# Dealing two rows of a weight matrix instead of one to the first few DMA engines, in a decode kernel on one core

## The chip, the core and the metric

The kernel runs on one core of one Trainium2 chip. The metric is the device time of one execution in microseconds (us), the median of several runs. Details below come from one execution that the hardware profiler recorded; its time axis starts with the first instruction of the program ("the span's start").

A core has five instruction streams: TensorE (PE in the profile, with its weight loads as PEld), VectorE (DVE), ScalarE (ACT), GpSimd (POOL) and SyncE (SP). DMA transfers are issued from SP and ACT here and are carried by the core's sixteen DMA engines, each of which works through its own share of every transfer.

## The reference: what is computed

A decode step for a batch of 8 tokens of width 512. An attention branch over a window of 2048 cached keys and values (8 key/value heads of 128, 32 query heads), and a gated unit whose result, once more through a gate, multiplies it:

```python
xn = layernorm(x)
s  = attention(xn @ wq, k_cache[:, :, -2048:], v_cache[:, :, -2048:]) @ wo
h  = sigmoid(xn @ w_gate) * (xn @ w_up)       # 8 x 1792
g  = silu(h @ w_down)                         # w_down: 1792 x 512
out = x + s * g
```

All inputs are bf16. The two caches' windows are 64 MB together, the weights about 13.5 MB; every byte is read once.

## The kernel before, in words

**One stream of loads.** Nearly all loads go through SP's queue `q0`, in an order that is written out by hand: the lists `todo` and `room` (lines 104 to 132) hold the tiles that are wanted and the buffers that are left, and `pump` issues a load as soon as its pool has room. The order is: x, `w_gate` (half of it on ACT's queue), `w_up`, `w_down` as tile `wd_sb`, `wq` in two tiles, the rest of `w_down` as `wd_part`, then 16 tiles of keys and 16 of values of 2 MB each (`k_sb`, `v_sb`), and last `wo` in five pieces of 12, 8, 6, 4 and 2 rows per partition (line 205). Each full load spreads its 128 partitions over the sixteen DMA engines, eight partitions to an engine. Keys and `wq`, `wo` share a pool of five buffers, values and the gated unit's weights one of four.

**The last weights of the gated unit.** `w_down` has 1792 rows of 512 bf16, 1 KB each. Seen as (p r) with 14 rows to a partition, rows 1 to 13 of every partition are loaded as one tile of 13 KB per partition (`want_rows("wd_sb", ..., FT, SD, FT)`, line 194, SD = 1). Row 0 of every partition, 128 rows in all, is loaded on its own by `want_part` (lines 179 to 192) into `wd_part`, a tile of 64 partitions x 3 rows in the values' pool. GpSimd first zeroes the tile (L183); then three transfers (L187) fill it, described by `PARTS` (lines 175 and 176): two with 60 rows whose source has 5 as its outermost size, and one with 8 rows and 4 outermost. The three are called "the dealt rows" below.

**The gated unit in order of work.** `hidden` (line 291) makes gate and up projections on PE; h_sb (L312) and its 32x32 transposed hT_sb (L320) follow on DVE. As the dealt rows lie on other partitions than the rest, h has to be put on those partitions too: three matmuls with 0/1 matrices `sel_part` (L327; made on DVE at L277 and L280) give hP_ps, and L335 copies it to hP_sb. Then 16 matmuls (L348) add up h @ w_down into w_ps, 13 on `wd_sb` and three on `wd_part`, in four row groups of PE by turns. The tail of that branch is L358 to L375. PE then makes q (L385, L404) and starts on the keys.

**Attention.** For each of 16 key tiles PE transposes 64 blocks (L481), DVE copies them out of PSUM (L486), PE makes the scores (L500); softmax, the turning of the probabilities (L571) and the products with the values (L597) are woven in by the table `tasks` (line 658). The output projection comes last: 20 rows of `wo` through part_ps (L719), then into fin_ps (L733); DVE multiplies and adds (L748, L750), SP stores the result (L751).

Of the kernel before, what the change touches and what calls it, by code (L numbers as in the profile page):

```python
# [10 lines left out]
def kernel(  # L11
# [13 lines left out]
    nc = tc.nc  # L25
    P = 128
    B, _, D = A_x.shape
    _, Hkv, Sk, Dh = A_k_cache.shape
# [20 lines left out]
    bf16 = mybir.dt.bfloat16  # L49
    f32 = mybir.dt.float32  # L50
# [8 lines left out]
    vpool = ctx.enter_context(tc.tile_pool(name="vpool", bufs=4))  # L59
    ktpool = ctx.enter_context(tc.tile_pool(name="ktpool", bufs=3))  # L60
    ppool = ctx.enter_context(tc.tile_pool(name="ppool", bufs=2))
    consts = ctx.enter_context(tc.tile_pool(name="consts", bufs=1))
    work = ctx.enter_context(tc.tile_pool(name="work", bufs=1))
    small = ctx.enter_context(tc.tile_pool(name="small", bufs=2))
    ps_t = ctx.enter_context(
        tc.tile_pool(name="ps_t", bufs=4, space=bass.MemoryType.PSUM)
    )
# [6 lines left out]
    ps_m = ctx.enter_context(  # L74
        tc.tile_pool(name="ps_m", bufs=1, space=bass.MemoryType.PSUM)
    )
    ctx.enter_context(tc.manual_schedule())


# [27 lines left out]
    def later(tag, f):  # L107
        todo.append((tag, f))
# [11 lines left out]
    def want_rows(name, w, tag, per, r0, r1):  # L120
        def f():
            t = load_rows(w, tag, per, r0, r1, name)
            for r in range(r0, r1):
                weights[(name, r)] = t[:, r - r0, :]

        later(tag, f)
# [13 lines left out]
    Z = 32  # L140
# [26 lines left out]

    A = 5  # L170
    SD = 1
    SX = 3
    HP = P // 2
    NA = 4 * A
    PARTS = ((0, NA, 0, SX, 0, A), (Z, NA, 0, SX, SX * NA, A))
    PARTS += ((Z + NA, P - 2 * SX * NA, 0, 1, 2 * SX * NA, 4),)
    d_room = []

    def want_part(w, per):
        def f():  # L180
            d = vpool.tile([HP, SX, SD, w.shape[1]], bf16, name="wd_part", tag="v")
            d_room.append(d)
            nc.gpsimd.memset(d[:], 0.0)  # L183
            for p0, n, x0, x1, s0, a in PARTS:
                m = n * (x1 - x0)
                src = w.rearrange("(y r) n -> y (r n)", r=per)[s0 : s0 + m]
                q0.dma_start(  # L187
                    out=d[p0 : p0 + n, x0:x1].rearrange("p x r n -> p (x r n)"),
                    in_=src.rearrange("(y a) n -> a y n", a=a)[:, :, : SD * w.shape[1]],
                )  # L190

        later("v", f)

    want_rows("wd_sb", B_w_down, "v", FT, SD, FT)
    for i in range(2):
        want_rows("wq_sb", A_wq, "k", KT, 2 * i, 2 * i + 2)
    want_part(B_w_down, FT)
    order = [(b, i) for b in range(B) for i in range(NQ)]
    AHEAD = 3
# [5 lines left out]
    for t0, t1 in ((0, 12), (12, KS), (KS, 26), (26, 30), (30, RT)):  # L205
# [4 lines left out]
    ident = consts.tile([P, P], bf16, name="ident")  # L210
# [6 lines left out]
        out=perm[:].rearrange("k (l p) -> k l p", l=G),  # L217
        in_=ident[:].rearrange("k (p l) -> k l p", l=G),
# [13 lines left out]
        out=rstd[:], in_=mv[:, 1:2], func=AF.Sqrt, bias=eps_t[:], scale=1.0  # L232
# [4 lines left out]
        out=xn_bf[:],  # L237
# [8 lines left out]
    for kt in range(KT):  # L246
        nc.tensor.transpose(  # L247
            out=xnT_ps[:, kt, :],
            in_=xn_bf[:].rearrange("b (p kt) -> b kt p", kt=KT)[:, kt, :],
# [11 lines left out]
    for t in p_buf:  # L261
        nc.vector.memzero(t[:])
    oP_sb = work.tile([P, RT, Z], bf16, name="oP_sb")
    nc.vector.memzero(oP_sb[:])

    NDQ = Dh // RT
    own_q = consts.tile([P, NDQ], f32, name="own_q")
    nc.vector.reduce_sum(
        out=own_q[:], in_=ident_f[:].rearrange("k (h q) -> k q h", q=NDQ), axis=AX.X
    )  # L270
    sel_z = consts.tile([P, Z], f32, name="sel_z")
    nc.vector.reduce_sum(
        out=sel_z[:], in_=ident_f[:].rearrange("k (j z) -> k z j", z=Z), axis=AX.X
    )

    sel_part = consts.tile([P, SX, HP], bf16, name="sel_part")
    nc.vector.memzero(sel_part[:])  # L277
    for p0, n, x0, x1, s0, a in PARTS:
        for x in range(x0, x1):
            nc.vector.tensor_copy(  # L280
                out=sel_part[:, x, p0 : p0 + n].rearrange("k (a e) -> k a e", a=a),
                in_=ident[:, s0 : s0 + n * (x1 - x0)].rearrange(
                    "k (e x a) -> k x a e", x=x1 - x0, a=a
                )[:, x - x0],
            )

    FC = F // NB

    def hidden(name):
# [21 lines left out]
        out=h_sb[:].rearrange("k t p -> k p t"),  # L313
# [5 lines left out]
    hT_sb = work.tile([P, FT, Z], bf16, name="hT_sb")  # L319
    nc.vector.transpose(  # L320
        out=hT_sb[:].rearrange("k t z -> k (t z)"),
        in_=h_sb[:].rearrange("k t p -> k (t p)"),
    )

    hP_ps = ps_t.tile([HP, SX, SD * Z], f32, name="hP_ps", tag="t")
    for x in range(SX):
        nc.tensor.matmul(  # L327
            hP_ps[:, x, :],
            lhsT=sel_part[:, x, :],
            rhs=hT_sb[:, :SD, :].rearrange("p t z -> p (t z)"),  # L330
            start=True,
            stop=True,
        )
    hP_sb = work.tile([HP, SX, SD * Z], bf16, name="hP_sb")
    nc.vector.tensor_copy(out=hP_sb[:], in_=hP_ps[:])  # L335
    down = [(hT_sb[:, t, :], weights[("wd_sb", t)]) for t in range(SD, FT)]
    for x in range(SX):
        top = max(p0 + n for p0, n, x0, x1, _, _ in PARTS if x0 <= x < x1)
        down += [
            (hP_sb[:top, x, Z * r : Z * (r + 1)], d_room[0][:top, x, r, :])  # L340
            for r in range(SD)
        ]

# [2 lines left out]
    for t, (h, w) in enumerate(down):  # L346
# [3 lines left out]
            lhsT=h,  # L350
            rhs=w,
            start=(t < NB),
            stop=(t >= len(down) - NB),
            tile_position=(0, Z * j),
            skip_group_check=True,
# [4 lines left out]
    for j in range(NB):  # L360
        nc.tensor.matmul(
            b_ps[Z * j : Z * (j + 1), :],
            lhsT=sel_z[:],
            rhs=w_sb[:, 0, j * P : (j + 1) * P],
            start=True,
            stop=True,
            tile_position=(0, Z * j),
            skip_group_check=True,
# [12 lines left out]
    for kt in range(KT):  # L381
        for x in range(Hkv // JQ):
            for j in range(JQ):
# [3 lines left out]
                    lhsT=xnT_sb[:, kt, :],  # L387
                    rhs=weights[("wq_sb", kt)][:, g * rep * Dh : (g + 1) * rep * Dh],
                    start=(kt == 0),
                    stop=(kt == KT - 1),  # L390
                    tile_position=(0, Z * j),
                    skip_group_check=True,
# [3 lines left out]
    for x in range(Hkv // JQ):  # L396
        src = q_ps[x][:].rearrange("k (r d) -> k r d", r=rep)
# [4 lines left out]
    for x in range(Hkv // JQ):  # L402
        for r in range(rep):
            nc.tensor.transpose(  # L404
                out=qT_ps[:, x, r, :], in_=q_bf[:, x, r, :], identity=ident[:]
            )
        nc.vector.tensor_copy(
            out=qm_sb[:, :, x * JQ : (x + 1) * JQ, M0 : M0 + rep],
            in_=qT_ps[:, x].rearrange("d r (j z) -> d z j r", z=Z)[:, ::S],
# [11 lines left out]
    for i in range(NQ):  # L421
        nc.vector.tensor_copy(
            out=turn_rows[:].rearrange("k (i j l r) -> k i j l r", i=NQ, j=NJ, l=G)[
                :, i
            ],
            in_=ident[:].rearrange("k (l j i r) -> k i j l r", i=NQ, j=NJ, l=G)[:, i],
        )
        nc.vector.reduce_sum(
            out=sel_den[:, i * Hh : (i + 1) * Hh].rearrange("k (l r) -> k l r", l=G),
            in_=ident_f[:].rearrange("k (l j i r) -> k i l r j", l=G, j=NJ, i=NQ)[:, i],  # L430
            axis=AX.X,
        )
    for e in range(2):
        nc.vector.reduce_sum(
            out=sel_out[:, e, :].rearrange("k (i h) -> k i h", i=NQ),
            in_=ident_f[:].rearrange(
                "k (i m e h) -> k e i h m", i=NQ, m=NJ // 2, e=2
            )[:, e],
# [6 lines left out]

    sel_res = consts.tile([P, Hq, NDQ], f32, name="sel_res")
    nc.vector.tensor_tensor(
        out=sel_res[:],
        in0=sel_out[:, 0, :].unsqueeze(2).to_broadcast([P, Hq, NDQ]),
        in1=sel_out[:, 1, :].unsqueeze(2).to_broadcast([P, Hq, NDQ]),  # L450
        op=ALU.add,
    )
    sel_sum = consts.tile([P, Hq, NDQ], f32, name="sel_sum")
    nc.vector.tensor_copy(
        out=sel_sum[:], in_=sel_den[:].unsqueeze(2).to_broadcast([P, Hq, NDQ])
# [261 lines left out]
    for t in range(KS):  # L717
# [3 lines left out]
            lhsT=oP_sb[:, t, :],  # L721
            rhs=weights[("wo_sb", t)],
            start=(t < NB),
            stop=(t >= KS - NB),
            tile_position=(0, Z * j),
            skip_group_check=True,
# [16 lines left out]
    for t in range(KS, RT):  # L743
# [8 lines left out]
        out=out.flatten_outer_dims().rearrange("b (j c) -> j b c", c=P),  # L752
        in_=y_bf[::S, :],
# [31 lines left out]
```

## Time and profile before

| what | value |
|---|---|
| median of 3 runs | 199.87 us (199.56 to 200.12) |
| the profiled execution, its own time | 199.72 us |
| its span, first to last instruction | 198.0 us |
| outside the span | 1.7 us |
| TensorE clock granted, mean | 0.972 of full speed |
| PE busy | 152.7 us, 77% of the span, 2133 matmuls |
| DVE busy | 122.2 us, 62% |
| ACT busy | 37.6 us, 19% |
| POOL busy | 3.0 us, 1% |
| bytes moved by DMA | 81.32 MB, a mean of 411 GB/s |

The page's chain of work that ended last gives DMA 57% of the span and PE 34%. The busy share of PE is a mean over stages: for the first 34 us it waits mostly for weights.

Besides instructions, the trace keeps each DMA packet (start, duration, bytes, queue) and each update of a semaphore. A packet here is one contiguous run of bytes of a transfer on one DMA engine. A transfer tells that it has landed by one update of its semaphore from each DMA engine that carried a part of it, after that engine's last packet; the instruction that needs the data waits for all of them. The packets' records don't name the engine, but on one engine each begins 3 to 4 ns before the one ahead of it ends, so that sixteen strands can be followed through the whole run. Times of packets and of landings differ by a constant: a landing is seen about 0.3 us after the packet.

### The profile page before, as it was taken

What the parts mean: (1) busy time and instruction counts of PE and PEld (TensorE: products, weight loads), DVE (VectorE), ACT (ScalarE), POOL (GpSimd) and SP (SyncE); (2) the same over time, 40 slices, a digit from 0 to 9 for tenths busy, and PEclk for the clock granted to TensorE, in tenths of its full rate; (3) what the DMA queues carried; (4) which work ended last, traced back from release to release, by engine and by line L of the source; (5) the groups of instructions that cost most, each with busy time, mean ns of one, the idle gap of its engine ahead of it and who ended that gap; (6) DMA issues with size and microseconds to landing.
All of it is one profiled execution on the core that took longest, in us unless ns stands there. A gap on an engine that the chain in (4) does not pass through costs nothing.

```text
span 198.0 us, 4772 instructions
## 1 busy us (share of the span) xinstructions
PE 152.7 (77%) x2133; PEld 103.3 (52%) x2133; DVE 122.2 (62%) x234; ACT 37.6 (19%) x91; POOL 3.0 (1%) x11
## 2 busy tenths in 40 slices
PE   0434038799979999989798969996989797898552
PEld 0111014677666677656565646674657565566421
DVE  3764002999978679758675937687858674852301
ACT  3200011000720610240024000600140033082010
POOL 5000000000000000000000000000000000000000
PEclk9999999999999999999999969999999999999975
DMA  6999999999999999999999999999999999999980
GB/s 207 433 438 428 428 443 427 434 424 422 430 427 434 427 434 427 427 430 427 427 427 435 427 430 430 422 434 424 430 427 434 427 434 430 427 424 422 421 341 10
DMA packets 6441, 81.32 MB, mean 411 GB/s; under 512 B 782, under 2 KB 918, under 8 KB 1558
## 3 DMA queue, kind: packets, MB, share of 16 engines
q1 hardware_dynamic: 6242, 80.10, 95.0%
q10 hardware_dynamic: 180, 0.93, 1.4%
q8 instruction: 16, 0.26, 0.5%
q14 instruction: 3, 0.02, 0.0%
HBM read 81.02 MB, written 0.01 MB: 409 GB/s over the span
## 4 chain that ended last, share of the span: by engine, by line
DMA 57%; PE 34%; ACT 3%; DVE 3%; SPq 1%; issue 1%
DMA k_sb<-in_A_k_cache_dram 33%; PE kT_ps L481 17%; DMA wo_sb<-in_A_wo_dram 11%; DMA wd_part<-in_B_w_down_dram 10%; PE o_ps L597 6%; PE s_ps L500 5%; DMA wg_sb<-in_B_w_gate_dram 3%; ACT p_buf L548 2%; PE pT_ps L571 2%; PE q_ps L385 1%; DVE kT_sb L486 1%; SPq L99 1%; ACT L548 1%; PE fin_ps L733 1%; PE qT_ps L404 0%
## 5 line engine op out<-in xcount | busy, mean ns | idle before, releaser
L486 DVE COPY kT_sb<-kT_ps 128x1024 bf16<-128x1024 bf16 x128 | 85.1, 686 | 30.8 <-PE kT_ps L481 30.1
L481 PE MATMUL kT_ps<-perm,k_sb 128*128 128x128 bf16 x1024 | 75.8, 221 | 10.1 <-DMA k_sb<-in_A_k_cache_dram 10.1
L481 PEld LDWEIGHTS <-k_sb 128*128 128x128 bf16 x1024 | 59.1, 99 | 29.8 <-issue 16.2
L597 PE MATMUL o_ps<-v_sb,pT_sb 128*32 128x256 bf16 x512 | 39.7, 276 | 1.6 <-DVE o_sb L618 0.9
L500 PE MATMUL s_ps<-kT_sb,qm_sb 128*32 128x512 bf16 x256 | 25.8, 393 | 1.9 <-DVE kT_sb L486 1.9
L597 PEld LDWEIGHTS <-pT_sb 128*32 128x32 bf16 x512 | 21.9, 96 | 10.2 <-issue 3.5
L548 ACT ACTIVATE p_buf<-s_ps,nb 32x512 bf16<-32x512 f32 x32 | 21.7, 678 | 0.5
L541 ACT COPY nb<-m_ps 128x1 f32<-128x1 f32 x8 | 1.3, 159 | 87.0 <-PE m_ps L535 87.0
L571 PE MATMUL pT_ps<-turn_rows,p_buf 128*128 128x128 bf16 x128 | 10.9, 230 | 1.5 <-ACT p_buf L548 1.5
L564 DVE COPY pT_sb<-pT_ps 128x1024 bf16<-128x1024 bf16 x14 | 9.6, 687 | 3.9 <-PE pT_ps L571 3.9
L500 PEld LDWEIGHTS <-qm_sb 128*32 128x32 bf16 x256 | 6.7, 93 | 8.8 <-issue 2.4
L571 PEld LDWEIGHTS <-p_buf 128*128 128x128 bf16 x128 | 9.3, 150 | 3.4 <-ACT p_buf L548 2.1
L613 ACT ACTIVATE o_odd<-o_ps,own_col 128x128 f32<-128x128 f32 x8 | 2.9, 368 | 28.5 <-PE o_ps L597 28.4
L375 DVE TENSOR_TENSOR gg_sb<-sigb,b_ps 128x128 f32<-128x128 f32 x1 | 0.3, 289 | 12.0 <-ACT sigb L371 12.0
L348 PE MATMUL w_ps<-wd_part,hP_sb 52*32 52x512 bf16 (+1 forms) x3 | 0.6, 597 | 8.1 <-DMA wd_part<-in_B_w_down_dram 8.1
L548 ACT ACTIVATION_READ_ACCUMULATOR p_buf<-s_ps,nb 32x1 f32 x32 | 5.9, 184 | 0.0
L515 DVE TENSOR_REDUCE st<-s_ps 128x1 f32<-128x512 f32 x8 | 5.5, 681 | 0.5 <-PE s_ps L500 0.5
L618 DVE SCALAR_TENSOR_TENSOR o_sb<-o_ps,own_col,o_odd 128x128 f32<-128x128 f32 x8 | 2.7, 339 | 3.5 <-ACT o_odd L613 3.5
L348 PEld LDWEIGHTS <-hP_sb 52*32 52x32 bf16 (+1 forms) x3 | 0.1, 97 | 9.0 <-issue 9.0
L640 DVE SCALAR_TENSOR_TENSOR own<-m_ps,inv,own_q 128x128 f32<-128x128 f32 x8 | 2.8, 346 | 3.1 <-PE m_ps L631 3.1
L247 PE MATMUL xnT_ps<-ident,xn_bf 8*128 8x8 bf16 x4 | 0.3, 174 | 5.4 <-DVE xn_bf L236 5.4
L295 PEld LDWEIGHTS <-xnT_sb 128*32 128x32 bf16 x32 | 1.1, 119 | 6.3 <-issue 5.8
(80 smaller groups left out, 67.9 us busy)
## 6 DMA issues: line engine op xcount, KB each, us to landing
k_sb<-in_A_k_cache_dram SPq DMA_DIRECT2D x16, 2048.0 KB, 30.3
v_sb<-in_A_v_cache_dram SPq DMA_DIRECT2D x16, 2048.0 KB, 27.1
wq_sb<-in_A_wq_dram SPq DMA_DIRECT2D x2, 2048.0 KB, 20.2
wu_sb<-in_B_w_up_dram SPq DMA_DIRECT2D x1, 1792.0 KB, 10.4
wd_sb<-in_B_w_down_dram SPq DMA_DIRECT2D x1, 1664.0 KB, 13.9
wo_sb<-in_A_wo_dram SPq DMA_DIRECT2D x1, 1536.0 KB
wo_sb<-in_A_wo_dram SPq DMA_DIRECT2D x1, 1024.0 KB, 20.4
wg_sb<-in_B_w_gate_dram ACTq DMA_DIRECT2D x1, 896.0 KB
```

The costliest lines, as they stand in the source:

```text
L99: q0.dma_start(out=t[:], in_=w.rearrange("(p r) n -> p r n", r=per)[:, r0:r1, :])
L481: nc.tensor.transpose(out=kT_ps[:, c, :], in_=k_sb[:, j * CU + h * CH + c, :], identity=perm[:],)
L486: nc.vector.tensor_copy(out=kT[(b, u)][:, h * CH : (h + 1) * CH, :], in_=kT_ps[:])
L500: nc.tensor.matmul(s_ps[b][NR * l : NR * (l + 1), :], lhsT=qm_sb[:, b, i * G + l, o : o + Z], rhs=t[:, :, PG * l : PG * (l + 1)], start=(u ...
L515: nc.vector.reduce_max(out=st[b][:], in_=s_ps[b][:], axis=AX.X)
L548: nc.scalar.activation(out=p_buf[b % 2][rows, :, l, :], in_=s[rows, :].rearrange("k (c p) -> k p c", p=PG), func=AF.Exp, bias=nb[rows, :], ...
L564: copy(out=pT[b][:, h * CH : (h + 1) * CH, :], in_=pT_ps.pop(h)[:])
L571: nc.tensor.transpose(out=pT_ps[h][:, c, :], in_=p_buf[b % 2][:, :, :, h * CH + c].rearrange("k p l -> k (p l)"), identity=turn_rows[:],)
L597: nc.tensor.matmul(o_ps[rows, b % 2, :].rearrange("k (e d) -> k e d", e=2), lhsT=pT[b][:, c, rows], rhs=v[:, m, c], start=(c == 0), stop=( ...
L613: nc.scalar.mul(out=o_odd[:], in_=o_ps[:, b % 2, Dh:], mul=own_col[:, 1:2])
L618: nc.vector.scalar_tensor_tensor(out=o_of[b // 2][:, b % 2, :], in0=o_ps[:, b % 2, :Dh], scalar=own_col[:, 0:1], in1=o_odd[:], op0=ALU.mul ...
L640: nc.vector.scalar_tensor_tensor(out=own[:], in0=m_ps[:, b % 2, P : 2 * P].rearrange("p (q t) -> p q t", q=NDQ), scalar=inv[y][:, b % 2 : ...
```

## The change

Two rows instead of one are taken out of every partition's share of `w_down` (SD = 2). `wd_sb` now has rows 2 to 13, 12 KB per partition. Rows 0 and 1, 256 rows of 1 KB, are dealt by two transfers instead of three: 192 rows in 96 pairs to a tile of 48 partitions (6 outermost in the source), and 64 rows in 32 pairs to a tile of 16 partitions (2 outermost). Each partition gets two pairs, a pair being one run of 2 KB. The tiles have a pool of their own and no padding, so that nothing is zeroed first. On PE two selecting matmuls stand for each tile, four in all instead of three, with two copies out of PSUM instead of one; and the sum for w_ps has 12 + 4 + 4 matmuls instead of 13 + 3. The 0/1 matrices are made by two copies, earlier in DVE's order, instead of by a memset and seven copies. The values' pool still counts a buffer for `wd_part` (`later("v", f)`), though the tile no longer lies in it.

```diff
+    d_pool = ctx.enter_context(tc.tile_pool(name="d_pool", bufs=1))
...
-    A = 5
-    SD = 1
-    SX = 3
-    HP = P // 2
-    NA = 4 * A
-    PARTS = ((0, NA, 0, SX, 0, A), (Z, NA, 0, SX, SX * NA, A))
-    PARTS += ((Z + NA, P - 2 * SX * NA, 0, 1, 2 * SX * NA, 4),)
+    SD = 2
+    PE = P // 16
+    SHARES = ((6, 0), (2, 6 * PE * SD))
     d_room = []
 
     def want_part(w, per):
         def f():
-            d = vpool.tile([HP, SX, SD, w.shape[1]], bf16, name="wd_part", tag="v")
-            d_room.append(d)
-            nc.gpsimd.memset(d[:], 0.0)
-            for p0, n, x0, x1, s0, a in PARTS:
-                m = n * (x1 - x0)
-                src = w.rearrange("(y r) n -> y (r n)", r=per)[s0 : s0 + m]
+            for a, s0 in SHARES:
+                n = a * PE
+                t = d_pool.tile([n, SD, SD, w.shape[1]], bf16, name=f"wd_part{a}")
+                src = w.rearrange("(y r) n -> y (r n)", r=per)[s0 : s0 + n * SD]
                 q0.dma_start(
-                    out=d[p0 : p0 + n, x0:x1].rearrange("p x r n -> p (x r n)"),
-                    in_=src.rearrange("(y a) n -> a y n", a=a)[:, :, : SD * w.shape[1]],
+                    out=t[:].rearrange("p u r n -> p u (r n)"),
+                    in_=src.rearrange("(y a) n -> a y n", a=a)[
+                        :, :, : SD * w.shape[1]
+                    ],
                 )
+                d_room.append((t, n, a, s0))
...
+    sel_part = []
+    for _, n, a, s0 in d_room:
+        sel = consts.tile([P, SD, n], bf16, name=f"sel_part{n}")
+        nc.vector.tensor_copy(
+            out=sel[:].rearrange("k u (a p) -> k u a p", a=a),
+            in_=ident[:, s0 : s0 + n * SD].rearrange(
+                "k (p u a) -> k u a p", u=SD, a=a
+            ),
+        )
+        sel_part.append(sel)
...
-    sel_part = consts.tile([P, SX, HP], bf16, name="sel_part")
-    nc.vector.memzero(sel_part[:])
-    for p0, n, x0, x1, s0, a in PARTS:
-        for x in range(x0, x1):
-            nc.vector.tensor_copy(
...
-    hP_ps = ps_t.tile([HP, SX, SD * Z], f32, name="hP_ps", tag="t")
-    for x in range(SX):
-        nc.tensor.matmul(
...
     down = [(hT_sb[:, t, :], weights[("wd_sb", t)]) for t in range(SD, FT)]
+    for (d, n, a, s0), sel in zip(d_room, sel_part):
+        ps = ps_t.tile([n, SD, SD * Z], f32, name="hP_ps", tag="t")
+        for u in range(SD):
+            nc.tensor.matmul(
+                ps[:, u, :],
+                lhsT=sel[:, u, :],
+                rhs=hT_sb[:, :SD, :].rearrange("p t z -> p (t z)"),
+                start=(u == 0),
+                stop=True,
+                skip_group_check=True,
+            )
+        hP_sb = work.tile([n, SD, SD * Z], bf16, name=f"hP_sb{n}")
+        nc.vector.tensor_copy(out=hP_sb[:], in_=ps[:])
         down += [
-            (hP_sb[:top, x, Z * r : Z * (r + 1)], d_room[0][:top, x, r, :])
+            (hP_sb[:, u, Z * r : Z * (r + 1)], d[:, u, r, :])
+            for u in range(SD)
             for r in range(SD)
         ]
```

More of the change, by code (lines that the diff above doesn't have):

```diff
@@ L274 @@
     )
-    sel_part = consts.tile([P, SX, HP], bf16, name="sel_part")
-    nc.vector.memzero(sel_part[:])
-    for p0, n, x0, x1, s0, a in PARTS:
-        for x in range(x0, x1):
-            nc.vector.tensor_copy(
[L281 to L285, printed above, removed]
     FC = F // NB
@@ L323 @@
     )
-    hP_ps = ps_t.tile([HP, SX, SD * Z], f32, name="hP_ps", tag="t")
-    for x in range(SX):
-        nc.tensor.matmul(
[L328 to L335, printed above, removed]
-    down = [(hT_sb[:, t, :], weights[("wd_sb", t)]) for t in range(SD, FT)]
-    for x in range(SX):
-        top = max(p0 + n for p0, n, x0, x1, _, _ in PARTS if x0 <= x < x1)
+    down = [(hT_sb[:, t, :], weights[("wd_sb", t)]) for t in range(SD, FT)]
+    for (d, n, a, s0), sel in zip(d_room, sel_part):
[11 more added lines that the diff above has]
+        nc.vector.tensor_copy(out=hP_sb[:], in_=ps[:])
         down += [
-            (hP_sb[:top, x, Z * r : Z * (r + 1)], d_room[0][:top, x, r, :])
+            (hP_sb[:, u, Z * r : Z * (r + 1)], d[:, u, r, :])
+            for u in range(SD)
             for r in range(SD)
```

## The prediction, on record before the changed kernel ran

> **What bounds the kernel now.** I read the page's slices first: are the DMA engines ever idle?
>
> ```profile
> PEclk9999999999999999999999969999999999999975
> DMA  6999999999999999999999999999999999999980
> GB/s 207 433 438 428 428 443 427 434 424 422 430 427 434 427 434 427 427 430 427 427 427 435 427 430 430 422 434 424 430 427 434 427 434 430 427 424 422 421 341 10
> ```
>
> From the second slice to the last but one the sixteen DMA engines are busy over 90% at a steady 420 to 440 GB/s; only start and end are thinner. Next the chain of work that ended last, at its end, and the time order there:
>
> ```profile
> 170.81 22.57 DMA wo_sb<-in_A_wo_dram
> 193.38 0.04 issue
> 193.42 1.02 PE fin_ps L733 x20
> 194.44 0.02 issue
> 194.47 0.30 DVE prod L748
> 194.77 0.02 issue
> 194.79 0.29 DVE y_bf L750
> ```
>
> ```profile
> 194.02 0.13 PEld L733 LDWEIGHTS <-oP_sb 128*32 128x32 bf16 x7 [0.17 <-issue]
> ```
>
> `wo` comes last. Its fourth piece lands at 193.38 and frees 16 matmuls of L733; the fifth lands, by its semaphore, at 193.97, and the last eight start at 194.02. From there to the end of the span are 4.0 us that the change doesn't touch. So the end is when the **slowest** DMA engine has carried its last part, and PE only follows.
>
> How even are the engines? The landings of the fifth piece, one update for each engine (us):
>
> ```
> 190.51 190.67 191.12 191.55 191.68 191.79 192.61 193.33
> 193.37 193.41 193.47 193.50 193.55 193.56 193.84 193.97
> ```
>
> Seven engines are done 1.4 to 3.5 us early, nine lie within 0.64 us. Why, the packets tell. One of 16384 bytes takes 0.607 us, start to start, nearly without exception, so an engine is late by what it carries besides. The queues of the page name the other traffic:
>
> ```profile
> q1 hardware_dynamic: 6242, 80.10, 95.0%
> q8 instruction: 16, 0.26, 0.5%
> q14 instruction: 3, 0.02, 0.0%
> ```
>
> The q8 packets are 16 KB of instructions each, at 33.3, 45.0, 54.5 us and so on to 184.5, after the first one for every 124 to 135 matmuls: PE's program. Each puts the engine that it falls on back by 1.41 us. Following the sixteen strands from 29.5 us on (all first key tiles landed), eight engines take them in a fixed rotation, two each, 2.83 us. The q14 packets in the stretch are 8 KB: at 47.8 and 124.0 (126 DVE instructions apart, so DVE's) both on one engine, X, 0.84 us each; at 106.5 on another, L, 0.55 us. Phase at 29.5 plus these delays gives all sixteen landings above within 0.08 us. The dealt rows are carried by five engines, four with 26 packets of 1 KB and one with 24; none of the five takes a q8 packet. They are the landings 191.55, 191.68, 191.79, 192.61 (L) and 193.33 to 193.41 (X). X and L are both of the four with 26. The early 190.51, 190.67 and 191.12 are the three engines with neither dealt rows nor q8 packets; the rest are the eight q8 engines.
>
> **The change part by part.** First the DMA, which is the whole sum. Packet steps, from the packets' records: 13312 bytes 0.494 us, 12288 bytes 0.456, 2048 bytes 0.080, 1024 bytes 0.042.
>
> - Every engine carries eight rows of `wd_sb`: 8 x (0.494 - 0.456) = **0.30 us less**.
> - The dealt rows before: 26 x 0.042 = 1.09 us on four engines, 24 x 0.042 = 1.01 on the fifth.
> - After: 192 KB over six engines, 16 packets of 2 KB each, 1.28 us; 64 KB over two, another 16, so 2.56 us on those. That the number of engines is the outermost size is seen before: 5, 5 and 4 late semaphore updates for outermost sizes 5, 5 and 4, and the four were among the five. I take it that the first two, four, five, six engines are nested in the same way and number them 0 to 15.
>
> Sum for each engine: 0 and 1: -0.30 + 2.56 - 1.09 = **+1.16 us**; 2 and 3: -0.30 + 1.28 - 1.09 = -0.12; 4: -0.03; 5: -0.30 + 1.28 = **+0.98**; 6 to 15: **-0.30**.
>
> If engine 5 is one of the three early ones and X is 2 or 3: the eight q8 engines end at 193.97 - 0.30 = 193.67 or before; X at 193.40 - 0.12 = 193.28; engines 0 and 1, at most L's 192.61 + 1.16 = 193.77, else 192.95; engine 5 at most 191.12 + 0.98 = 192.10. The end moves by -0.20 to -0.30. PE has to follow: its last wait before L733 is for the fourth piece, and all landings of late engines move together.
>
> The rest lies beside the stream:
>
> - GpSimd's memset goes (L183, 1.38 us, before the identity matrix). What it delayed, LayerNorm's chain, is ahead of PE's wait for `w_gate` (landing 7.75); nothing. DVE: one memset (0.14) and seven copies (0.18 each) go, two copies and one 0.25 us copy of hP come; DVE waits 1.88 us for `w_up` just behind them.
> - SP issues two transfers instead of three, at 5.7 to 8.4 us, 0.7 to 1.0 us each. The semaphores rotate over eight, so each later issue waits for the landing of another, earlier transfer. The queue is many transfers deep; nothing, at most 1 us of earlier issue that no one needs. The values' first four tiles find buffers that are free earlier, same answer.
> - PE waits longer for the dealt rows:
>
> ```profile
> 26.93 0.61 PE L348 MATMUL w_ps<-wd_part,hP_sb 60*32 60x512 bf16 x3 [8.10 <-DMA wd_part<-in_B_w_down_dram]
> 31.68 0.60 SPq L89 DMA_DIRECT2D v_sb<-in_A_v_cache_dram  x1
> ```
>
> The last dealt row lands at 26.79 before; after, 1.16 us later at worst. The four late matmuls take 0.6 to 0.8 us instead of 0.61. Behind them on PE stand b_ps, q and the key transposes, and SP's fourth key tile waits for q to free its buffer (issued at 31.1). So that issue comes some 1.1 us later. Cover: at 31.1 the first key tile is just landing (31.48) and the two behind it last until 41.23, ten us of stream. PE itself waits 22.7 us later on for keys (10.1 for matmuls, 12.6 for weight loads, partly the same time), so 1.1 us are made up. If that cover were gone, the whole 1.1 us would show.
> - One more 16 KB of instructions? Five matmuls more, the next fetch would come some 126 matmuls behind that at matmul 2028 of 2133, so after the last one. Nothing. DVE has five instructions fewer; its two fetches stay.
> - PE's clock is at half from 190.45 on. The 48 matmuls of L733 lie in it before and after; where that border falls differently, I bound it at ±0.25 us (half of the last 24 matmuls' 0.5 us), and take nothing.
>
> [...]
>
> **Rivals.**
>
> 1. *X is one of the two doubly loaded engines* (slower). The place: DVE's two fetches and 32 packets on one engine. X ends at 193.33 to 193.41 before, so 194.49 to 194.57 after, 0.52 to 0.60 later than 193.97: **200.4 us**. It decides as soon as X is 0 or 1, since X has 0.6 us of room and gets 1.16. For it: X is one of four with 26 packets, two of which are doubled, so by count 1 in 2. Against it no row speaks; that I go down to about 1 in 3 is a guess, that DVE's is not the first of the fetch queues to be given an engine.
> 2. *Engine 5 is a q8 engine* (slower). Six of those eight end at 193.33 to 193.56, +0.98 gives 194.31 to 194.54, 0.34 to 0.57 later; the other two give 0.85 to 0.98. Centre **200.4 us**, worst 200.9. For it: of eleven engines without dealt rows eight are q8 engines. Against: the eight leave out all five first engines, so they are hardly scattered; as a block of eight it reaches down to 5 in one of four places only, and not if it is the upper half.
> 3. *The transfers spread otherwise than over 6 and 2 engines.* Over all sixteen: 8 x 0.080 = 0.64 - 0.30 = +0.34 on the q8 engines, **200.2 us**. Against it the 5, 5 and 4 updates of now.
> 4. *The later PE start drains the stream.* Up to +1.1, **201.0 us**; against it the ten us of cover.
>
> **How the numbers follow.** Against the profiled execution's own 199.72 us (198.0 of span and 1.7 around it) the sum is 199.42 to 199.52. The median of the runs shown is 0.15 above that execution, so I put the change on the median: 199.87 - 0.25 = **199.6 us**. Chances: forecast 0.47, rival 1 0.28, rival 2 0.15 (with or without 1), rivals 3 and 4 0.05, the rest, such as the clock's border, 0.05. The likeliest case's own range is 199.3 to 199.9 (runs differ by ±0.3); with rivals 1 and 2 the range is 199.25 to 200.6. About 0.3%, 0.6 us, is what a measurement of this kernel can tell from no change. The forecast lies within it, and rivals 1 and 2 at +0.5 lie near its upper edge: two in five of them, and rival 4, come out beyond. So slower 0.25, within 0.64, faster 0.11.
>
> **What would show it.** In the profile after: the first dealt transfer with six late updates and the second with two; 128 packets of 2048 bytes more and none of 1024 from the dealt rows; PE's wait for the dealt rows up by about 1.1 us; still 16 q8 packets. Among the sixteen last landings two should have moved from about 191.6 to 192.8 and one from about 191 to 192, with the last at about 193.7. If the last stands at 194.5 with one engine alone behind the rest, rival 1 or 2 holds: alone in having two 8 KB fetches, rival 1; alone with q8 packets, rival 2. A slice of the stream below nine tenths between 30 and 60 us would mean rival 4. The prediction is wrong altogether if the landings stay as even as I say and the time still moves by over 0.6 us.

## The result, and the profile after

The changed kernel takes **201.28 us** (median of 6 runs, 200.90 to 201.61), the kernel before 199.86 us beside it (199.56 to 200.20): a ratio of **1.0068 [1.0052, 1.0084]**. So it is slower by 0.7%, where 199.6 us and no measurable change were forecast, and it lies above the forecast's range of 199.25 to 200.6. The profiled execution took 201.27 us, 199.5 of them span.

The page of the changed kernel, its slices (PE's clock, the DMA engines' busy share, what they moved; a slice is 5 us) and its queues:

```profile
PEclk9999999999999999999999999999999789999975
DMA  6999999999999999999999999999999999999970
GB/s 216 434 444 424 416 330 437 427 424 430 429 427 427 424 440 430 424 421 434 434 434 425 421 434 437 425 427 417 434 434 440 417 424 427 437 437 418 412 325 10
...
q1 hardware_dynamic: 6236, 80.10, 94.9%
q8 instruction: 16, 0.26, 0.5%
q14 instruction: 3, 0.02, 0.0%
```

The DMA line is as full as before. But the sixth slice (24.9 to 29.9 us) moved 330 GB/s, where before it had 443 and its neighbours have 416 and 437. At 430 GB/s the missing 100 GB/s over 5 us are 1.2 us of stream. The instruction fetches are as many as before: 16 of PE's, three of 8 KB.

The chain of work that ended last:

```profile
173.43 21.61 DMA wo_sb<-in_A_wo_dram
195.04 0.04 issue
195.08 0.62 PE fin_ps L730 x16
195.70 0.02 issue
195.72 0.43 PE fin_ps L730 x8
196.15 0.02 issue
196.18 0.30 DVE prod L745
```

The end has the form that it had before, with the fourth piece of `wo` at 195.04 instead of 193.38. The sixteen landings of the fifth piece (us):

```
191.42 191.43 191.83 192.67 193.26 194.23 194.31 194.33
194.36 194.40 194.53 194.64 194.72 195.09 195.44 195.68
```

The prediction looked for two readings: one engine alone behind the rest (rival 1 or 2), or a thin slice between 30 and 60 us (rival 4). Neither is there. The body that stood at 193.33 to 193.56 now stands at 194.23 to 194.72, so nearly every engine is late, by about a microsecond. Three stand behind the body, at 195.09 to 195.68; which they are is told with the steps of the prediction.

Windows of the trace (time, then the busy time and count of PE, PEld, DVE, ACT and POOL, the granted clock, the DMA engines' busy share, GB/s), first the kernel before, then the changed one:

```profile
24.00:30.00 6.00, 2.10 (x22) 0.82 (x25) 0.29 (x1) 0.86 (x2) 0.00 (x0) 1.00 1.01 429
```

```profile
24.00:30.00 6.00, 0.73 (x8) 0.30 (x7) 0.00 (x0) 0.00 (x0) 0.00 (x0) 1.00 1.02 339
30.00:60.00 30.00, 25.79 (x362) 18.15 (x358) 22.68 (x47) 5.98 (x13) 0.00 (x0) 1.00 1.00 427
```

Read the last two columns together: the engines are busy 100% of both windows, yet from 24 to 30 us they move 339 GB/s instead of 429. A packet that takes longer counts as busy. The 90 GB/s over 6 us are 0.54 MB, **1.26 us** of stream. From 30 us on the stream is full again.

Those six microseconds are when the dealt rows travel. Packet by packet:

| | dealt packets | slow (over 1.1 x the first ones) | 16384-byte packets, 23 to 36 us |
|---|---|---|---|
| before | 128 of 1024 bytes, mean 0.046 us | 0 | one beyond 0.62 us, 0.5 us lost (an instruction fetch) |
| after | 128 of 2048 bytes, 0.084 to 0.204 us, mean 0.126 | 89 | 81 beyond 0.62 us, up to 1.20, 15.8 us lost |

The dealt packets lose 5.4 us in all, the others 15.8; together 21 us over sixteen engines, **1.3 us each on average**, as the window gave. The engines without dealt rows are not spared: five such strands, which can be followed through the window, lost 1.11 to 1.23 us each. The first five to eight dealt packets of an engine still take 0.084 us; between 25.02 and 25.16 us all six engines slow down, whatever number each had written. The sixteen dealt packets of one strand, in ns:

```
84 84 84 84 84 84 84 139 169 173 153 146 125 105 134 153
```

### The profile page after: what moved, and what is told of

It reads as the page before. It is cut to its first block, busy times and chain, and to the rows that moved or that the text cites. A ratio compares the mean times of both kernels' runs of the same rounds, so it can differ in the third digit from the quotient of the medians.

```text
span 199.5 us, 4773 instructions
## 1 busy us (share of the span) xinstructions
PE 152.4 (76%) x2138; PEld 103.2 (52%) x2138; DVE 122.0 (61%) x229; ACT 37.7 (19%) x91; POOL 1.4 (1%) x10
## 4 chain that ended last, share of the span: by engine, by line
DMA 56%; PE 35%; ACT 3%; DVE 3%; SPq 1%; issue 1%
DMA k_sb<-in_A_k_cache_dram 31%; PE kT_ps L478 18%; DMA wd_part<-in_B_w_down_dram 12%; DMA wo_sb<-in_A_wo_dram 11%; PE o_ps L594 6%; PE s_ps L497 5%; DMA wg_sb<-in_B_w_gate_dram 2%; ACT p_buf L545 2%; PE q_ps L382 1%; PE pT_ps L568 1%; DVE kT_sb L483 1%; SPq L100 1%; ACT L545 1%; PE fin_ps L730 1%; SPq L182 0%
## 5 line engine op out<-in xcount | busy, mean ns | idle before, releaser
L345 PE MATMUL w_ps<-wd_part,hP_sb 48*32 48x512 bf16 (+1 forms) x8 | 1.2, 598 | 10.9 <-DMA wd_part<-in_B_w_down_dram 10.9
L355 ACT COPY w_sb<-w_ps 128x512 f32<-128x512 f32 x1 | 0.6, 587 | 21.3 <-PE w_ps L345 21.3
```

## The experiments

After the result there was one new fact, slow packets while the dealt rows are on their way, and three explanations. **The place**: an engine writes to other partitions than before. The kernel before dealt 20 partitions over five engines from 0 on, and 20 more from 32 on, so engine i filled 4i to 4i+3 and 32+4i to 35+4i with all but the last 8 dealt rows. The changed kernel deals 48 partitions in order over six engines, so engine i fills 8i to 8i+7. The trace has no addresses; that is read from the order of the elements in the code. Below, 4i to 4i+3 and 32+4i to 35+4i are called the own blocks of engine i, or its home, and any others out of place. That is a name for the order of before (continued for further engines) and no more: which partitions an engine fills in a full load, no run shows. **The source**: runs of 2 KB read with another step than runs of 1 KB. **The loads alone**: engines 0, 1 and 5 carry more, as counted, and the rest is chance.

### e1: the same rows by the same engines, written to their own blocks

```diff
-                n = a * PE
-                t = d_pool.tile([n, SD, SD, w.shape[1]], ...)
+                n = a * PE // 2
+                t = d_pool.tile([Z + n, SD, SD, w.shape[1]], ...)
+                nc.vector.memzero(t[:])
+                for g in range(2):
+                    s1 = s0 + g * n * SD
                     q0.dma_start(
-                    out=t[:]...
+                        out=t[Z * g : Z * g + n]...
```

Each share goes in two transfers, to partitions from 0 on and from 32 on; the selecting matrices follow.

> The changed kernel, with each share of the dealt rows split over two transfers so that an engine writes partitions 4i to 4i+3 and 32+4i to 35+4i (tiles of 56 and 40 partitions, zeroed on DVE first) instead of 8i to 8i+7. Bytes, packet size (2 KB), engines (6 and 2) and loads are those of the changed kernel. Theory A (where the packets are written is what slows them and everything beside them): the 2048-byte packets take 0.084 us nearly all, the 16384-byte packets beside them 0.611, the last dealt row lands at about 28.0, the last landing at 193.7 if the loads were told rightly (199.6 us) or at 194.5 if one of the doubly loaded or the sixth engine is a burdened one (200.4 us). Theory B (the source, 2 KB runs 14 KB apart, is what slows them): packets as slow as now, 0.1 to 0.19 us, and 201.3 us. Theory C (only the uneven loads, my recorded sum, with a misjudged engine): 201.3 us too, but with fast packets.

Measured: 200.36 us against 199.66, **1.0034 [1.0023, 1.0044]**. Of the 128 packets none is slow, all take 0.084 us; of the 16384-byte packets one (the fetch). The window and PE's two waits for the dealt rows:

```profile
24.00:30.00 6.00, 2.26 (x20) 0.79 (x21) 0.00 (x0) 0.86 (x2) 0.00 (x0) 1.00 0.99 418
```

```profile
26.36 0.62 PE L355 MATMUL w_ps<-wd_part,hP_sb 56*32 56x512 bf16 x4 [7.84 <-DMA wd_part<-in_B_w_down_dram]
...
27.68 0.62 PE L355 MATMUL w_ps<-wd_part,hP_sb 40*32 40x512 bf16 x4 [0.70 <-DMA wd_part<-in_B_w_down_dram]
```

In the changed kernel the same two lines read:

```profile
27.54 0.62 PE L345 MATMUL w_ps<-wd_part,hP_sb 48*32 48x512 bf16 x4 [9.15 <-DMA wd_part<-in_B_w_down_dram]
...
29.89 0.61 PE L345 MATMUL w_ps<-wd_part,hP_sb 16*32 16x512 bf16 x4 [1.73 <-DMA wd_part<-in_B_w_down_dram]
```

The last landings:

```
190.07 190.46 190.77 191.46 191.48 192.85 193.08 193.12
193.16 193.17 193.26 193.31 193.45 193.47 193.79 194.39
```

The slow packets are gone, and with them 1.29 us at the last landing. The engine still reads the same rows in the same order, so the source falls. And now the picture that the prediction asked for is there: the body moved to 193.08 to 193.79 and **one engine alone** stands behind it, at 194.39. Which one, its strand tells: it carried 16 dealt packets and two of PE's fetches (65.3 and 143.3 us). Engines 0 to 4 took none of PE's in the kernel before, so it is engine 5, rival 2. X, with the 8 KB fetches at 50.1 and 123.9, has 16 dealt packets, not 32: it is engine 2 or 3, and rival 1 is false.

### e2: the kernel before, with its dealt rows written out of place

```diff
-    PARTS = ((0, NA, 0, SX, 0, A), (Z, NA, 0, SX, SX * NA, A))
+    PARTS = ((0, 2 * NA, 0, SX, 0, A),)
```

One transfer of 120 rows to partitions 0 to 39, so 8i to 8i+7 for engine i; packets of 1 KB, loads as before.

> The kernel before, with its two transfers of 60 rows made one of 120 rows to partitions 0 to 39, so that each of the five engines writes partitions 8i to 8i+7 instead of 4i to 4i+3 and 32+4i to 35+4i. Loads (24 packets of 1 KB, 26 with the third transfer) and the third transfer are unchanged; one transfer fewer is issued. Theory A: the 1024-byte packets get slower than their 0.046 us, the 16384-byte packets beside them slower than 0.611, for as long as the dealt rows last; 120 KB against the changed kernel's 256 KB, so about half its loss: 0.5 to 0.8 us, 200.4 to 200.7 us. Theory B: nothing changes, 199.9 us, packets at 0.046.

Measured: 199.99 us against 199.66, 1.0016 [1.0007, 1.0026].

```profile
24.00:30.00 6.00, 1.80 (x19) 0.76 (x23) 0.29 (x1) 0.86 (x2) 0.00 (x0) 1.00 1.00 393
```

30 of 128 packets are slow (up to 0.105 us instead of 0.046), and the 16384-byte packets lose 7 us; before, 0.5 us, at one fetch. So the place, with the packets, the loads and the rest of the kernel as before (one transfer fewer), makes a loss. Of 24 runs the first 17 to 22 of an engine are still fast, and the loss (0.33 us) is smaller than the 0.5 to 0.8 expected: half the bytes, of which most go before the slowing begins.

### e3: the changed kernel, reading blocks of rows instead of every sixth

```diff
-                    in_=src.rearrange("(y a) n -> a y n", a=a)[...
+                    in_=src.rearrange("(a y) n -> a y n", a=a)[...
```

The selecting matrices follow.

> The changed kernel, with the source dealt in blocks: engine i reads 16 neighbouring row pairs (14 KB apart) instead of every sixth (84 KB apart) or every second one; destinations, packet sizes and engines unchanged. Theory A: no change, 201.3 us and 2048-byte packets of 0.1 to 0.19 us. Theory B: the pattern in HBM is another one, so packets and time change, down to 199.6 to 200.4 us if the conflict is gone, or up if it is worse.

Measured: 201.40 us against 199.66, 1.0083 [1.0068, 1.0098]; 311 GB/s in the window, packets up to 0.366 us. The edit did more than was meant. Each of the two dealt transfers landed with sixteen semaphore updates (25.83 to 27.71 and 26.64 to 27.98 us) instead of six and two: read in blocks, the 96 and the 32 pairs each follow one another at a single step, and all sixteen engines shared them, eight runs each if the shares are equal. So this run doesn't separate the source from the engines. It shows that the loss returns with other engines and even loads, while most runs are still written out of place by the order of the elements: the dealt packets lose 9.4 us and the 16384-byte ones 16.7, and the time is 201.40 us where rival 3 gave 200.2 for such a spread by its loads alone. That the source isn't the cause rests on e1 beside e4 and e5 below, which read the same rows in the same order.

### e4 and e5: other places that are not the engine's own

```diff
e4 -  out=t[Z * g : Z * g + n]...     e4 +  out=t[Z * g + 4 : Z * g + 4 + n]...
e5 -  out=t[Z * g : Z * g + n]...     e5 +  out=t[2 * Z * g : 2 * Z * g + n]...
```

Both from e1, with tiles and selecting matrices made to fit. In e4 every engine writes four partitions further on, into the blocks called the next one's; in e5 the first half of the packets stays at home and the second goes to partitions from 64 on.

> [...] Loads as in e1_own_ports (200.4 us). [...] Own-block theory (any write outside an engine's own block is slow by itself): all 128 dealt packets slow, 201.3 us as in the changed kernel. Source theory: 200.4 us, all fast, as the source is that of e1_own_ports.

> [...] If only the blocks of neighbouring engines or of the lower 64 partitions get in each other's way: all fast, 200.4 us as e1_own_ports.

Measured: e4 201.87 us, 1.0117 [1.0104, 1.0131]; e5 201.65 us, 1.0106 [1.0093, 1.0119], both against 199.51. Window 369 and 344 GB/s; slow dealt packets 61 and 41; the 16384-byte packets lose 10.9 and 16.7 us. Both lose again, and more than I expected: one engine lands last alone once more, at 196.00 and 195.91. Its strand carries dealt rows and two of PE's fetches (57.1 and 133.9 us in e4, 35.7 and 113.2 in e5), so it is engine 5 again, late by its load and by the place. From e1 these two differ in the partitions alone, and the tiles' heights with them; the four transfers, the zeroing, the loads and the source are the same. So the place makes the loss. The numbers of slow packets, 61 and 41 of 128, fit no simple count: if each packet out of place were slow by itself, e4 would have 128 and e5 64. Out of place is slow, but how the slowness is shared stays open.

### e7 and e8: only one of the two shares at home; e9: a control

```diff
+    SHARES = ((6, 2, 0), (2, 1, 6 * PE * SD))   # e7: first share at home
+    SHARES = ((6, 1, 0), (2, 2, 6 * PE * SD))   # e8: second share at home
+    SHARES = ((6, 1, 0), (2, 1, 6 * PE * SD))   # e9: neither
```

The middle number is how many transfers a share goes in. All three zero their tiles on DVE as e1 does; e9 is the changed kernel with this zeroing alone.

> As e1_own_ports, but only the first share (192 rows on six engines) goes to each engine's own blocks; the second (64 rows on two engines, partitions 0 to 15) is written as in the changed kernel. [...] If the first share's place alone decides, it is e1_own_ports' 200.4 us.

> The mirror of e7_own_first: the first share to partitions 0 to 47 as in the changed kernel, the second to the engines' own blocks. [...] The two losses over e1_own_ports, of this and of e7_own_first, should add up to the changed kernel's.

> A control: the changed kernel with nothing but the zeroing on DVE that e1_own_ports and its kin add (two tiles and the 0/1 matrices). All theories: that is beside the stream, 201.3 us as the changed kernel, the same slow packets.

| | us | against 199.50 | GB/s, 24 to 30 us | slow dealt packets | lost by 16 KB packets, us |
|---|---|---|---|---|---|
| e7 | 200.60 | 1.0056 [1.0039, 1.0073] | 426 | 8 | 1.5 |
| e8 | 201.65 | 1.0107 [1.0092, 1.0122] | 350 | 80 | 12.2 |
| e9 | 201.27 | 1.0091 [1.0075, 1.0106] | 336 | 88 | 15.2 |

The control agrees with the changed kernel (201.28 us, 339 GB/s, 89 packets), so zeroing isn't it. Nearly the whole loss is the first share's, 192 KB by six engines; the second, 64 KB by two, costs nearly nothing when the first is at home: e7's last landing is 194.40, e1's was 194.39. Its time, 200.60, is 0.2 us above the 200.4 expected if the first share's place alone decides, though so few packets are slow. The losses don't add up as expected: e8 keeps all of the loss, with its last landing at 195.67 (195.68 in the changed kernel).

### e6: at home, and engine 5 left out

```diff
+    SHARES = ((5, 2, 3, 0), (2, 1, 1, 120))
```

The numbers are engines, transfers, runs to a partition and the first row pair. Five engines carry 24 runs each (in two transfers, at home), the first two 4 more; engine 5 none.

> Own blocks as in e1_own_ports, but the dealt rows lie on five engines (24 runs of 2 KB each) and 4 runs more on the first two, so that the sixth engine carries none; fewer on the first two (28 instead of 32). If e1_own_ports stands at 200.36 us because its sixth engine also fetches PE's instructions (rival 2 of the prediction): the lone last landing (194.39 there, 0.6 us behind the rest) is gone; the last engine is the one with DVE's two fetches, 193.38 - 0.30 - 1.09 + 1.92 = 193.9 in the terms of the kernel before, the fetch engines at 193.7, so 199.6 to 199.8 us, at the kernel before or 0.1 under it. If the lone engine is one of the first two: 28 runs instead of 32 take 0.3 us off, 194.1 alone behind the rest, 200.1 us.

Measured: 200.01 us against 199.51, 1.0031 [1.0020, 1.0043].

```profile
24.00:30.00 6.00, 2.12 (x20) 0.75 (x21) 0.00 (x0) 0.59 (x1) 0.00 (x0) 1.00 1.01 429
```

```
189.99 190.46 190.53 192.00 192.43 192.47 193.05 193.08
193.16 193.18 193.20 193.23 193.30 193.39 193.41 193.97
```

No slow packet, and the engine alone behind the rest is now X (fetches at 49.0 and 122.8 us), at 193.97 where 193.9 was expected. So the sums by engine hold when the place is right. But X with 24 runs ends where the kernel before ended, and the time is 0.2 us above the 199.6 to 199.8 that I gave it. The time alone would also fit the other branch (200.1, one of the first two last); the strands decide. From the last landing to the store's issue both take 1.1 us; the store and what follows take 3.1 us of span here and 2.9 in the profile of before. No version was found that beats the kernel before.

## Why the prediction was wrong, by its steps

- **The step that failed: "2048 bytes 0.080"**, and with it the sum by engine. The number came from `wo`'s last piece, a full load of 128 packets, and was used for packets that a few engines write out of place. It is a step from start to start, a duration of 0.084, and at home it holds (e1). Out of place the packets took 0.126 on average, and, what was not asked at all, they slowed the other packets: the engines lost 1.3 us on average, the ten with no dealt rows too. The prediction gave each of six engines a load and the other ten -0.30; it had no term for where a packet is written. At the last landing this term is 194.39 to 195.68, **+1.29 us** (e1 to changed). Both are landings of the same engine: the last strand of the changed kernel has 16 dealt packets and two of PE's fetches (75.1 and 154.9 us), so it is engine 5. The two ahead of it, at 195.44 and 195.09, are L, now with 32 dealt packets, and X with 16.
- **Engine 5: +0.98.** The size is right, the engine was wrong. It was put down as one of the three early engines, with rival 2 at 0.15 ("the eight leave out all five first engines, so they are hardly scattered"). It is one of the eight with PE's fetches. The landing, 194.39 in e1, is within the 194.31 to 194.54 that rival 2 gave. That is 0.42 us beyond 193.97, and e1's 200.36 us is close to its 200.4.
- **Engines 6 to 15: -0.30** holds: the body, 193.33 to 193.97 before, stands at 193.08 to 193.79 in e1, engine 5 left out.
- **X and L** hold, where the trace can say: X is engine 2 or 3 (rival 1 false). The two engines with 32 packets land at 192.85 (bound 192.95) and 193.45 in e1; the second has the 8 KB fetch at 107.4 us, so it is L, for which 193.77 was forecast.
- **Six and two late updates** hold (rival 3 false): the first dealt transfer has six between 27.06 and 27.49, the second two, 28.95 and 29.85. But the last was to come at 27.95, 1.16 after 26.79; in e1, at home, PE's last wait ends at 27.68, as counted; the other 2.2 us, to 29.89, are the place.
- **PE starts later, covered by ten us of stream** holds (rival 4 false): key transposes start at 36.66 instead of 34.21, and the stream from 30 to 60 us stays at 427 GB/s.
- **Instruction fetches, DVE, GpSimd at nothing**: 16 and three as counted, and e9 (201.27 us with the zeroing, 201.28 without) shows that work on DVE there doesn't matter.
- **PE only follows** is nearly at its limit now. In e9 the chain runs through PE and ACT from the landing of the second piece of `wo` (191.88 us), without a wait for the last three:

```profile
191.88 0.04 issue
191.92 1.07 PE part_ps L726 x8
192.99 0.02 issue
193.01 0.59 ACT part L736
193.61 0.04 issue
193.65 1.29 PE fin_ps L740 x32
```

All pieces are late alike, so PE is late with them; that adds nothing that I can tell apart.

In time, e1 is 1.0034 and the changed kernel 1.0068 (1.0091 in the control's comparison): engine 5's load makes a good third to a half, the place the rest. Of the 1.29 us at the last landing 0.9 show in the span (198.6 to 199.5 us), since the store and what follows took 2.7 us in the changed kernel's profile and 3.1 in e1's; why these differ is not shown.

**What could have been seen before.** The code of before has the offset `Z` = 32 and 20 partitions in each of two transfers, where one transfer of 40 would do. Writing down each dealing engine's partitions before and after would have shown that the change moves them, as it moves the rows and the packet size. No row of before prices a stretch of packets that go elsewhere (its last 8 dealt rows do, 2 KB an engine, and took 0.046 us like the rest), so both ends were open. An estimate from the packets' steps of before was possible: if each of 128 packets of 0.08 us puts another packet back by its own length, and waits as long itself, 10 us are lost by each kind. By the total, 20 us, that is near the 21 measured; by the split, 5.4 and 15.8, it is not.

All sixteen engines were late here, 1.3 us on average, but no run shows by which path.

## What to carry to other kernels

When a transfer is confined to a few engines, write down for each engine not only how many packets it carries but into which partitions, and where a version that runs at full pace has an order for them, keep it (here 4i to 4i+3 and 32+4i to 35+4i, at 429 GB/s). Padding and an extra transfer were cheaper here than a tight tile (200.36 us in e1 against 201.28). A duration taken from a row holds for the row's source, size and destination (2 KB took 0.084 us at home and 0.126 on average out of place): where the change alters the third, it is an unknown cost with two ends. And read the GB/s beside the DMA share: slowed packets look like full use (a share of 1.02 at 339 GB/s).

## What the runs showed of the hardware that I had not expected

- 256 KB written out of place, 0.3% of the kernel's bytes, took the stream from 429 to 339 GB/s for six microseconds, on all sixteen engines: the first key tile's ten earliest landings are 30.91 to 31.43 us, in e1 29.48 to 30.34.
- The first packets out of place are fast, and then all dealing engines slow down nearly at once: in the changed kernel 0.64 us after the first dealt packet, within 0.13 us of each other, with 10 to 16 KB written by each; in e2 0.8 us after it, with 17 to 22 KB.
- Engines that carry none of the dealt rows were slowed too: the five of their strands that can be followed lost 1.11 to 1.23 us each in the changed kernel.
- One of PE's fetch engines is within the first six engines (the last strand of e1: 16 dealt packets, and PE's fetches at 65.3 and 143.3 us), and DVE's falls on engine 2 or 3 (X: 16 dealt packets, and the 8 KB fetches at 50.1 and 123.9 us). Neither could be had from the profile of before.
